# Linear attention into a gated Fourier filter: all inverse DFT tiles by one scheme, five output buffers and another order of work

## The chip, the cores and the metric

The kernel runs on one core of a Trainium2 chip. A core has a matrix engine (TensorE, PE in the profile; its weight loads are PEld), a vector engine (VectorE, DVE), a scalar engine (ScalarE, ACT), a general engine (GpSimd, POOL) and a queue engine (SyncE, SP) that here only issues DMAs. Each engine runs its instructions in the order in which it got them; between engines, semaphores hold an instruction back until its data is there or its buffer is free. PE writes into PSUM, eight banks of 128 x 512 fp32; DVE and ACT read it, POOL does not. The metric is the time of one execution in device microseconds: less is better.

## The reference

Eight batches with eight heads of 576 positions. The attention is linear: a feature map of exponentials, a sum over the keys, a quotient. Its output goes through three projections, one of which is convolved with a filter along the 576 positions (a product in the Fourier domain), and the gated product through a last projection.

```python
def phi(x):
    proj = np.einsum('bhsd,df->bhsf', x, w_phi)
    proj = proj - np.max(np.abs(proj), axis=-1, keepdims=True)
    return np.concatenate([np.exp(proj), np.exp(-proj)], axis=-1)
q_p, k_p = (phi(q), phi(k))
kv = np.einsum('bhsf,bhsd->bhfd', k_p, v)
z = np.sum(k_p, axis=2)
num = np.einsum('bhsf,bhfd->bhsd', q_p, kv)
den = np.einsum('bhsf,bhf->bhs', q_p, z)[..., None] + 1e-06
x = num / den                                   # -> [8, 576, 512]
...
proj = x @ w_proj                               # -> x1, x2, x3, 512 columns each
X2 = np.fft.rfft(x2, n=S, axis=1)
H = np.fft.rfft(filter_fft, n=S, axis=0)[None, :, :]
x2_conv = np.fft.irfft(X2 * H, n=S, axis=1)
y = x1 * x2_conv * x3
return (y @ w_out).astype(np.float32)
```

## The kernel before, in words

The whole order of work is written out by hand, as a text of some 1,480 words (`PLAN`, line 31). `run` (L1061) walks through it: each word names a method, its arguments (batch, tile, sometimes the engine) and, behind `@`, the first PSUM bank that it uses. No planner stands between: the words of one engine, in their order, are that engine's queue. A DMA stands in the queue of the engine that issues it: transposes (`trh`, `trx`, `trxt`) and nearly all stores (`st`) on SP, the loads of q, k, v and the weights (`load`, `loadh`, `w_load`) on POOL, between its arithmetic.

The batches run as a pipeline, several of them under way at a time. For one batch b:

- `load` brings q, k, v; `trh` transposes q and k by DMA. `Pk`, `Qn` (PE, L626, L633) project to the feature space, `maxk`, `maxq` (DVE, L707) take the largest absolute value, `ex` (ACT, L693) the two exponentials, `em` and `vs` (ACT L743; POOL or DVE L749) scale v. `Pq` projects q the other way round, `KV` (L753) sums over the keys, `NE` (L771) makes numerator and denominator, `rc` and `xn` (DVE, L792, L797) the quotient.
- `trx` transposes xn by DMA into xT for the projections. `f1` and `f2` (L844, L850) add and subtract its parts and `F` (L855) is the forward DFT into XF, copied out by `Fe`.
- `X2` (L892) projects in the Fourier domain, `Y1` (L899) multiplies by the filter into the tiles T0 to T4, `m3` (L909) adds two pairs of these.
- `X1`, `X3` (L940, L952) project in the position domain, `X1e` copies x1 out, `tm` (L958) multiplies by x3; the product stays in x1s.
- The inverse DFT goes by four tiles of 128 columns per batch, in one of two forms. `I` (L966) makes even and odd frequencies apart, three matmuls of 288 columns each, into two PSUM banks that stand side by side; `Ie` (ACT, L990) copies the first bank to SBUF (es), `Ip` and `Im` (DVE, L993) write the sum and the difference of es and the second bank to cv, and `ym` (L1038, POOL or DVE) multiplies cv by x1s into yT. `J` (L1021) makes the two halves of the result directly, five matmuls each, ten in all, for which it needs four further tables (`gen_neg`, `gen_ends`); `yj` (DVE, L1032) then multiplies both banks by x1s into yT in one instruction. 21 tiles go by I, 11 by J.
- `O` (L1046) is the last projection, by tiles c of a batch (c = 4 joins two batches), `Oe` copies it to an output buffer (o), and two `st` store that buffer's halves. `yt` (L1043) copies a remainder between two batches.

Buffers come in rings (`RING`, L25): a name with n buffers gives the n-th next writer the first buffer again, and it waits until its readers are done. `turn_of` (L228) hands out o, es and cv in the order in which the plan names their tiles: o has four buffers, es and cv two each. The words `wz` (L311) are matmuls on zeros, put where PE would otherwise stand still.

The end of the plan, with the last J, reads (L189 to L195):

```
X1e,ACT,7,1@5 Im,7,1@1 ym,POOL,7,0 J,7,2@6 tm,7,1@0 tm,7,2@4 ym,POOL,7,1 O,6,1@5 yj,7,2@6
Oe,ACT,6,1@5 O,7,2@6 yt,ACT,7 st,SP,6,1,1 O,7,1@7 Oe,ACT,7,2@6 st,SP,6,1,0 O,7,0@5 st,ACT,7,2,0
```

SP's queue around the second batch's transposes reads: `trh,q,4,1 st,0,0,0 trx,2,0 trx,2,1 trx,2,2 trx,2,3 trxt,2 st,0,3,0 st,0,3,1 st,0,0,1 trh,k,4,1 trh,q,4,0`. The output copies take their buffers in the order (0,3), (0,0), (0,1), (0,2), (1,0), (1,2), ...

Of the kernel before, what the change touches and what calls it, by code (L numbers as in the profile page):

```python
# [37 lines left out]
pt,k,0,0,1@3 sin,0 maxq,0,0@4 Pk,0,0@0 pte,ACT,k,0,0,1@3 pt,k,0,1,1@6 fa,POOL,1 pt,k,0,1,0@7
maxk,0,0@0 pte,ACT,k,0,1,1@6 Qn,0,2@4 pte,ACT,k,0,1,0@7 pte,DVE,q,0,1,1@2 maxq,0,2@4 Pk,0,1@6
Qn,0,3@2 ft,POOL fa,POOL,0 maxq,0,3@2 ex,k,m,0,0@0 wz,9@4 Qnt,0@4 ex,k,p,0,0@0 maxqt,0@4 Pk,0,2@2  # L40
maxk,0,2@2 ex,k,m,0,1@6 Pk,0,3@4 w_load,proj,1 rev@0 ex,k,p,0,1@6 maxk,0,3@4 mhi,0 ex,k,p,0,2@2
maxk,0,1@6 ex,k,m,0,2@2 one Pkt,0@6 mlo,DVE,0 ex,k,m,0,3@4 trm,0@2 wz,1@3 maxkt,0@6 trh,q,1,0
fb,0@0 trme,ACT,0@2 wz,12@3 em,m,0,0 ex,k,p,0,3@4 vs,POOL,m,0,0 Pq,0,1@2 trh,q,1,1 fb,1@0 em,p,0,0
exkt,m,0@6 Pq,0,2@4 exkt,p,0@6 ex,q,m,0,1@2 wz,25@0 trh,k,1,0 vs,POOL,p,0,0 ex,q,p,0,1@2 Qn,1,0@0
wz,14@6 trh,k,1,1 em,m,0,1 ex,q,p,0,2@4 maxq,1,0@0 Pq,0,3@2 w_load,proj,2 KV,0,0@6 ex,q,m,0,2@4
vs,DVE,m,0,1 em,p,0,1 ex,q,p,0,3@2 Ff,1@4 vs,POOL,p,0,1 KVe,DVE,0,0@6 Pk,1,1@0 ex,q,m,0,3@2
Ffe,DVE,1@4 Qn,1,3@6 ex,k,m,1,1@0 maxq,1,3@6 NE,0,1@4 Ff,0@2 w_load,proj,0 maxk,1,1@0 KV,0,1@6
Ffe,ACT,0@2 load,v,1 rc,0,1@4 ex,k,p,1,1@0 gen_ends,POOL Pq,0,0@2 xn,0,1@4 KVe,DVE,0,1@6 Qnt,1@4
trx,0,1 ex,q,m,0,0@2 Pk,1,0@0 maxqt,1@4 Ff,2@6 load,k,2 ex,q,p,0,0@2 maxk,1,0@0 NE,0,3@4 load,q,2
Ffe,ACT,2@6 NE,0,0@2 rc,0,3@4 ex,k,p,1,0@0 xn,0,3@4 NE,0,2@6 rc,0,0@2 Pqt,0@4 xn,0,0@2 ex,k,m,1,0@0  # L50
rc,0,2@6 ptx,0,3@2 f1,POOL,0,0,0 xn,0,2@6 exqt,p,0@4 ptx,0,0@3 Ff,3@0 exqt,m,0@4 ptxe,DVE,0,3@2
ptx,0,2@6 ptxe,DVE,0,0@3 f1,POOL,0,0,1 Ffe,ACT,3@0 Qn,1,2@4 ptxe,DVE,0,2@6 Pk,1,3@2 maxq,1,2@4
NEt,0@0 ex,k,m,1,3@2 f1,POOL,0,1,0 Pkt,1@6 exkt,m,1@6 rct,0@0 wz,27@4 maxk,1,3@2 f2,POOL,0,0,0
exkt,p,1@6 X1,0,0@5 Hl,ACT maxkt,1@6 H,0@4 f2,POOL,0,0,1 ex,k,p,1,3@2 xnt,0,0@0 H,2@6 xnt,0,1@0
He,DVE,0,0@4 f1,POOL,0,1,1 Qn,1,1@0 em,m,1,0 He,ACT,2,0@6 Pk,1,2@2 maxq,1,1@0 H,1@7 X1e,ACT,0,0@5
X1,0,3@6 ex,k,m,1,2@2 trh,k,2,0 He,DVE,0,1@4 X3,0,0@5 em,p,1,0 He,ACT,1,0@7 f2,DVE,0,1,1
vs,POOL,p,1,0 maxk,1,2@2 F,0,1@0 trh,k,2,1 X1e,ACT,0,3@6 X1,0,2@4 Fe,ACT,0,1@0 tm,0,0@5 H,4@6
em,m,1,1 f2,DVE,0,1,0 ex,k,p,1,2@2 X3,0,3@5 vs,POOL,m,1,0 X1e,DVE,0,2@4 trh,q,2,0 He,ACT,4,0@6
F,0,0@2 He,DVE,1,1@7 F,0,2@0 tm,0,3@5 Fe,ACT,0,0@2 H,3@4 trh,q,2,1 Fe,ACT,0,2@0 F,0,3@2
vs,POOL,m,1,1 He,ACT,3,1@4 Pk,2,0@0 KV,1,0@6 Fe,ACT,0,3@2 maxk,2,0@0 trxt,0 mhi,1 em,p,1,1  # L60
He,ACT,3,0@4 Pk,2,1@2 Xl,DVE,0 load,v,2 X2,0,2@5 ex,k,p,2,0@0 maxk,2,1@2 mlo,POOL,1 X2,0,1@4
KVe,ACT,1,0@6 load,q,3 late Y1,0,2@5 ex,k,p,2,1@2 trm,1@6 vs,POOL,p,1,1 X2,0,0@7 ex,k,m,2,0@0
trme,DVE,1@6 Y1,0,1@4 X2,0,4@5 ex,k,m,2,1@2 Pq,1,1@0 Y1,0,4@5 load,v,3 X2,0,3@4 ex,q,m,1,1@0
Y1,0,0@7 w_load,out Pkt,2@2 ex,q,p,1,1@0 X1,0,1@5 maxkt,2@2 load,k,3 Y1,0,3@4 X3,0,2@7 exkt,m,2@2
m3,POOL,0,0 exkt,p,2@2 Qn,2,1@0 X1e,ACT,0,1@5 tm,0,2@7 Pq,1,0@2 Pq,1,2@4 maxq,2,1@0 ex,q,m,1,0@2
X1t,0@7 X3t,0@6 ex,q,p,1,0@2 m3,DVE,0,1 X3,0,1@0 X1te,DVE,0@7 em,m,2,0 ex,q,p,1,2@4 tmt,0@6
NE,1,0@2 vs,POOL,m,2,0 tm,0,1@0 J,0,0@6 ex,q,m,1,2@4 rc,1,0@2 xn,1,0@2 NE,1,1@0 trx,1,0 yj,0,0@6
I,0,2@2 rc,1,1@0 Ie,0,2@2 I,0,1@6 xn,1,1@0 em,p,2,0 vs,POOL,p,2,0 Ie,0,1@6 Ip,0,2@2 trx,1,1
Pq,1,3@0 Im,0,1@6 KV,1,1@4 Im,0,2@2 ex,q,m,1,3@0 Ip,0,1@6 f1,DVE,1,0,1 Pk,2,2@6 ex,q,p,1,3@0
ym,POOL,0,1 J,0,3@2 maxk,2,2@6 KVe,ACT,1,1@4 NE,1,3@4 ym,POOL,0,2 ex,k,m,2,2@6 yj,0,3@2 NE,1,2@0  # L70
rc,1,3@4 KV,2,0@2 ex,k,p,2,2@6 rc,1,2@0 xn,1,3@4 f1,POOL,1,0,0 xn,1,2@0 trx,1,3 Pqt,1@6 Qn,2,0@4
exqt,m,1@6 f1,POOL,1,1,0 O,0,3@0 maxq,2,0@4 exqt,p,1@6 trx,1,2 O,0,0@1 KVe,ACT,2,0@2 f2,DVE,1,0,1
Oe,ACT,0,3@0 f1,DVE,1,1,1 Qn,2,3@2 trh,q,3,1 Oe,ACT,0,0@1 Qnt,2@4 f2,DVE,1,1,0 f2,POOL,1,1,1
NEt,1@6 maxq,2,3@2 O,0,1@1 trh,k,3,0 f2,POOL,1,0,0 rct,1@6 O,0,2@0 xnt,1,0@6 Oe,ACT,0,1@1 xnt,1,1@6
maxqt,2@4 Pk,2,3@2 trh,k,3,1 Oe,ACT,0,2@0 F,1,2@6 maxk,2,3@2 F,1,3@4 Fe,ACT,1,2@6 F,1,0@0 trh,q,3,0
Fe,ACT,1,3@4 X1,1,3@6 Fe,DVE,1,0@0 ex,k,m,2,3@2 Qn,2,2@4 st,SP,0,1,0 X1e,DVE,1,3@6 em,m,2,1 F,1,1@0
vs,POOL,m,2,1 trxt,1 maxq,2,2@4 X1,1,2@7 Fe,ACT,1,1@0 Qn,3,2@0 st,SP,0,1,1 mhi,2 X2,1,2@4
X1e,ACT,1,2@7 maxq,3,2@0 ex,k,p,2,3@2 load,q,4 X3,1,2@5 Y1,1,2@4 mlo,POOL,2 load,q,5 trm,2@2
X2,1,1@3 trme,ACT,2@2 em,p,2,1 tm,1,2@5 vs,POOL,p,2,1 Pq,2,0@1 Y1,1,1@3 Qn,3,0@4 Pq,2,1@6
ex,q,m,2,0@1 X3,1,3@0 maxq,3,0@4 ex,q,p,2,0@1 load,k,4 X1,1,0@3 ex,q,p,2,1@6 tm,1,3@0 Pq,2,2@4  # L80
ex,q,m,2,1@6 Pkt,3@0 X2,1,3@2 maxkt,3@0 X2,1,0@6 exkt,m,3@0 Y1,1,3@2 exkt,p,3@0 X1,1,1@7
ex,q,m,2,2@4 Y1,1,0@6 NE,2,1@0 X1e,ACT,1,1@7 X3,1,0@2 X1e,ACT,1,0@3 rc,2,1@0 m3,POOL,1,0 xn,2,1@0
ex,q,p,2,2@4 NE,2,0@6 tm,1,0@2 X1t,1@3 rc,2,0@6 Pqt,2@4 xn,2,0@6 X1te,ACT,1@3 Pq,2,3@0 exqt,p,2@4
Xl,DVE,1 Pk,3,1@2 f1,POOL,2,0,1 KV,2,1@6 trh,q,4,1 exqt,m,2@4 maxk,3,1@2 ex,q,p,2,3@0 f1,POOL,2,0,0
X2,1,4@4 st,SP,0,0,0 KVe,ACT,2,1@6 ex,q,m,2,3@0 trx,2,0 NE,2,2@6 m3,POOL,1,1 Y1,1,4@4 X3t,1@5
# [110 lines left out]
class Kernel:  # L196
# [807 lines left out]

    def gen_neg(self, eng):
        inv = self.at("inv")
        if eng == "ACT":
            self.nc.scalar.mul(inv[:, 6:8, :], inv[:, 2:4, :], -1.0)  # L1010
# [104 lines left out]
```

## Time and profile before

| | |
|---|---|
| median of 3 runs | 309.1 us (308.93 to 318.01) |
| span of the profiled execution | 311.6 us; no other time is given for this execution |
| busy in it: PE, DVE, ACT, POOL | 281.0, 268.6, 216.3, 203.8 us |
| mean granted clock of PE | 0.974 |
| moved by DMA | 40.2 MB |

The span runs from the first to the last instruction of one execution under the profiler. A row of a group names line, engine, operation, output and input tiles with their shapes and the count; behind the bar stand busy time and the mean of one in ns, and behind the second bar the idle time just before them and what ended it. A row of the timeline begins with start and length. A row of the chain of work has start, length and what it was. A row of the busy times by stage begins with its limits in us from the start. A matmul's length in a row is longer than what it takes of PE's time, since matmuls overlap in the array.

### The profile page before, as it was taken

The page shows a single profiled execution, that of the slowest core. Times are in us where ns is not written, and L with a number is a line of the kernel's source. Part 1 is how long each engine was busy: PE and PEld are TensorE (multiplying, and loading weights), DVE is VectorE, ACT ScalarE, POOL GpSimd, SP SyncE. Part 2 cuts the span into 40 slices and gives each one's busy share as a digit, 9 for nine tenths or more (in the row PEclk, how much of TensorE's full clock was granted, in tenths as well). Part 3 has the DMA queues.
Part 4 walks back from the last instruction along what each step waited for, and adds up shares of the span by engine and source line. Part 5 has one row for each costly group of instructions (what it writes and reads, how often), then busy time and mean ns, then how long its engine had stood idle before and what let it go on. Part 6 is the DMA issues. An engine that isn't in the chain of part 4 may idle for free.

```text
span 311.6 us, 10240 instructions
## 1 busy us (share of the span) xinstructions
PE 281.0 (90%) x4331; PEld 205.3 (66%) x4360; DVE 268.6 (86%) x447; ACT 216.3 (69%) x345; POOL 203.8 (65%) x163
## 2 busy tenths in 40 slices
...
GB/s 162 235 203 159 136 202 193 105 190 133 91 164 204 94 110 170 116 160 107 114 198 82 131 160 153 172 175 160 84 117 4 56 93 69 19 110 21 1 115 192
DMA packets 72735, 40.20 MB, mean 129 GB/s; under 512 B 53040, under 2 KB 67504, under 8 KB 72688
## 3 DMA queue, kind: packets, MB, share of 16 engines
q1 hardware_dynamic: 57472, 22.62, 40.2%
...
q14 instruction: 13, 0.11, 0.1%
...
## 4 chain that ended last, share of the span: by engine, by line
PE 70%; DVE 12%; DMA 7%; ACT 5%; issue 3%; SPq 1%; POOL 0%; DVEq 0%; POOLq 0%
PE ps L919 16%; PE ps L897 10%; PE ps L1049 8%; PE ps L764 5%; PE ps L972 4%; PE ps L778 4%; DMA xT<-xn 4%; DMA out_dram<-o 3%; PE ps L1028 3%; PE ps L858 3%; PE ps L862 3%; PE ps L928 2%; DVE mq L707 2%; PE ps L665 2%; PE ps L638 2%
## 5 line engine op out<-in xcount | busy, mean ns | idle before, releaser
L919 PE MATMUL ps<-xT,wproj 128*128 128x256 bf16 x512 | 65.8, 275 | 4.3 <-DVE x1s L960 2.3
L919 PEld LDWEIGHTS <-wproj 128*128 128x128 bf16 x512 | 48.6, 98 | 14.5 <-issue 5.1
L707 DVE TENSOR_REDUCE mk<-ps 128x8 f32<-128x1024 f32 (+1 forms) x40 | 44.0, 1110 | 5.9 <-ACT HTo L295 2.2
L707 DVE TENSOR_REDUCE mq<-ps 128x8 f32<-128x1024 f32 (+1 forms) x40 | 44.0, 1110 | 5.5 <-PE ps L638 4.5
L749 POOL TENSOR_TENSOR vm<-vn,vm 128x1152 bf16<-128x1152 bf16 x14 | 30.4, 2178 | 18.2 <-ACT vm L743 18.2
L749 POOL TENSOR_TENSOR vp<-vn,vp 128x1152 bf16<-128x1152 bf16 x16 | 34.8, 2180 | 10.5 <-ACT vp L743 10.3
L911 POOL TENSOR_TENSOR T<-T,T 128x1024 bf16<-128x1024 bf16 x12 | 25.5, 2124 | 21.9 <-DVE T L907 21.8
L693 ACT ACTIVATE Ekp<-ps 128x1024 bf16<-128x1024 f32 x32 | 32.8, 1030 | 6.6 <-DVE mk L707 3.3
L1038 POOL TENSOR_TENSOR yT<-cv,x1s 128x576 bf16<-128x576 f32 x19 | 24.3, 1289 | 18.3 <-DVE x1s L964 12.8
L852 POOL TENSOR_TENSOR xf<-SD 128x512 bf16<-128x512 bf16 x27 | 31.2, 1170 | 6.7 <-DVE SD L846 5.3
L693 ACT ACTIVATE Ekm<-ps 128x1024 bf16<-128x1024 f32 x32 | 32.8, 1033 | 3.6 <-DVE mk L707 2.7
L693 ACT ACTIVATE Eqm<-ps 128x1024 bf16<-128x1024 f32 x32 | 32.9, 1034 | 3.1 <-PE ps L671 2.9
L1049 PE MATMUL ps<-wout,yT 128*128 128x512 bf16 x133 | 34.3, 385 | 0.7 <-issue 0.2
L693 ACT ACTIVATE Eqp<-ps 128x1024 bf16<-128x1024 f32 x32 | 32.5, 1031 | 3.4 <-PE ps L671 3.3
L846 POOL TENSOR_TENSOR SD<-xn 128x512 bf16<-128x512 bf16 x23 | 26.5, 1160 | 12.6 <-DVE xn L797 12.6
L897 PE MATMUL ps<-wproj,XF 128*128 128x512 bf16 x117 | 30.3, 380 | 0.7 <-issue 0.2
L295 ACT CAST x1s<-ps 128x512 bf16<-128x512 f32 (+1 forms) x30 | 16.0, 548 | 13.1 <-PE ps L928 8.4
L797 DVE TENSOR_TENSOR xn<-ps,r 128x512 bf16<-128x512 f32 x32 | 22.0, 689 | 1.1
L1049 PEld LDWEIGHTS <-yT 128*128 128x128 bf16 x144 | 13.4, 99 | 14.1 <-issue 0.6
L990 ACT COPY es<-ps 128x288 f32<-128x288 f32 x21 | 8.5, 404 | 20.3 <-PE ps L972 19.8
L960 DVE TENSOR_TENSOR x1s<-ps,x1s 128x512 bf16<-128x512 f32 x32 | 21.7, 683 | 0.6 <-ACT x1s L295 0.4
L778 PE MATMUL ps<-KVs,Eqp 128*128 128x65 bf16 x256 | 19.6, 192 | 2.2 <-DVE mq L707 0.6
(174 smaller groups left out, 692.3 us busy)
## 6 DMA issues: line engine op xcount, KB each, us to landing
...
```

What stands on the lines that cost most here:

```text
L693: self.nc.scalar.activation(e, p, AF.Exp, bias=0.0, scale=1.0 if g == "p" else -1.0)
L707: self.nc.vector.tensor_reduce(out=out, in_=src, axis=AX.X, op=ALU.max, apply_absolute_value=True)
L749: self.eng(eng).tensor_tensor(out=t[:, :, :, 0:64], in0=self.at("vn", b)[:, 2 * X:2 * X + 2], in1=t[:, :, :, 64:65].to_broadcast([128, 2, ...
L778: self.mm(self.pb(u, 65 * a, 65 * a + 65), E, KVs[:, u, v, s, :], start=(s == 0), stop=(s == 1))
L797: self.nc.vector.tensor_tensor(out=o, in0=n[:, :, :, 0:64], in1=self.at("r", 4 * b + v).to_broadcast([128, 2, 4, 64]), op=ALU.mult)
L846: self.eng(eng).tensor_tensor(out=o[:, :, 2 * i:2 * i + 2, :], in0=x[:, :, 0:2, :], in1=x[:, :, 2:4, :], op=ALU.subtract if i else ALU.add)
L852: self.eng(eng).tensor_tensor(out=o[:, :, 2 * i:2 * i + 2, :], in0=x[:, :, 0:4:2, :], in1=x[:, :, 1:4:2, :], op=ALU.subtract if i else ALU ...
L897: self.mm(self.pb(0), l, w[:, kt, 512:1024], start=(kt == 0), stop=(kt == 3))
L911: self.eng(eng).tensor_tensor(out=Y, in0=Y, in1=self.at(f"T{2 * e + 1}", b), op=ALU.add)
L919: self.mm(o[:, d], w[:, kt, f0 + 128 * m:f0 + 128 * m + 128], y[:, 1, ::-1, ::-1] if d else y[:, 0], start=(kt == 0), stop=(kt == 3))
L1038: self.eng(eng).tensor_tensor(out=self.at("yT", b)[:, m, 0:SEQ], in0=self.turn_of("cv", (b, m)).rearrange("p x h t -> p (x h t)"), in1=sel ...
L1049: self.mm(self.pb(0), y[:, kt, 128 * c:128 * c + 128], w[:, kt, :], start=(kt == 0), stop=(kt == 3))
```

## The change

All 32 inverse tiles go by I: J, yj and the two methods that make its tables go, `inv` shrinks from ten tables to six, and o gets a fifth buffer (four tables are 2,304 bytes of a partition, one such buffer 2,048). The plan is written anew: many words stand elsewhere, have other PSUM banks or another engine. The counts of words that change: I, Ie, Ip, Im 21 to 32; J, yj 11 to 0; gen_neg, gen_ends 1 to 0; ym on POOL 19 to 25, on DVE 2 to 7; Fe on ACT 26 to 20, on DVE 6 to 12; Oe on ACT 19 to 28, on DVE 17 to 8; X1e on ACT 24 to 26, on DVE 8 to 6; X1te on ACT 6 to 7; Xl on DVE 3 to 4; f1 on POOL 23 to 25, on DVE 9 to 7; f2 on POOL 27 to 26, on DVE 5 to 6; vs on POOL 30 to 31, on DVE 2 to 1; mlo on POOL 5 to 6; Ffe on DVE 1 to 2.

```diff
-RING = {..., 'r': 4, 'o': 4, 'kn': 2, ...}
+RING = {..., 'r': 4, 'o': 5, 'kn': 2, ...}
...
-X1e,ACT,7,1@5 Im,7,1@1 ym,POOL,7,0 J,7,2@6 tm,7,1@0 tm,7,2@4 ym,POOL,7,1 O,6,1@5 yj,7,2@6
-Oe,ACT,6,1@5 O,7,2@6 yt,ACT,7 st,SP,6,1,1 O,7,1@7 Oe,ACT,7,2@6 st,SP,6,1,0 O,7,0@5 st,ACT,7,2,0
...
+trh,k,4,0 st,SP,0,2,1 st,SP,0,3,0 st,SP,0,1,0 trx,2,1 trx,2,0 trh,q,4,1 trh,k,4,1 trx,2,2 trx,2,3
+trxt,2 st,SP,0,0,0 trh,q,4,0 st,SP,0,1,1 I,1,3@2 Pk,3,2@4 Pk,3,0@0 Ie,1,3@2 ex,k,m,3,2@4
...
+maxk,3,2@4 X1,2,1@3 O,1,0@2 Qn,3,3@6 F,2,0@0 O,1,2@4 yt,ACT,1 Oe,ACT,1,0@2 Fe,ACT,2,0@0 Oe,ACT,1,2@4
+X1e,DVE,2,1@3 maxq,3,3@6 Pk,3,3@0 X1,2,2@5 F,2,3@6 maxk,3,3@0 Fe,DVE,2,3@6 F,2,2@2 Fe,DVE,2,2@2
+O,1,3@4 F,2,1@6 Fe,DVE,2,1@6 em,m,3,0 em,p,3,0 X1e,ACT,2,2@5 ex,k,m,3,3@0 em,m,3,1 ex,k,p,3,3@0
...
+Y1,7,4@0 X2,7,3@1 Y1,7,3@1 O,6,2@3 X3,7,3@2 Oe,ACT,6,2@3 O,6,3@1 m3,DVE,7,1 tm,7,3@2 I,7,3@5
+Ie,7,3@5 Ip,7,3@5 Im,7,3@5 ym,POOL,7,3 I,7,1@3 Ie,7,1@3 Oe,ACT,6,3@1 Ip,7,1@3 Im,7,1@3 ym,DVE,7,1
+X1,7,2@2 I,7,0@0 Ie,7,0@0 I,7,2@5 Ie,7,2@5 X1e,ACT,7,2@2 X3,7,2@3 O,6,0@4 Oe,ACT,6,0@4 st,SP,5,0,0
+st,SP,5,1,1 st,SP,6,3,1 st,SP,6,3,0 st,SP,6,2,0 st,SP,6,2,1 st,SP,6,0,0 O,6,1@7 Oe,ACT,6,1@7
+st,SP,6,0,1 st,SP,6,1,1 st,SP,6,1,0 Ip,7,0@0 Im,7,0@0 ym,POOL,7,0 Ip,7,2@5 tm,7,2@3 Im,7,2@5
+ym,DVE,7,2 O,7,1@0 Oe,DVE,7,1@0 yt,DVE,7 O,7,2@3 Oe,ACT,7,2@3 st,ACT,7,1,0 st,ACT,7,2,0 O,7,3@1
+Oe,DVE,7,3@1 st,ACT,7,3,1 st,SP,7,1,1 st,SP,7,2,1 st,SP,7,3,0 O,7,0@7 Oe,ACT,7,0@7 st,ACT,7,0,1
+st,SP,7,0,0 O,7,4@2 Oe,DVE,7,4@2 st,ACT,7,4,0 st,SP,7,4,1
...
-        R("inv", [128, 10, 288], BF16)
+        R("inv", [128, 6, 288], BF16)
...
-    def gen_neg(self, eng):
...
-    def gen_ends(self, eng):
...
-    def J(self, b, m):
...
-    def yj(self, b, m):
```

The new plan's output copies take their buffers in the order (0,3), (0,0), (0,2), (0,1), (1,0), (1,2), (1,3), ... SP's stores of (0,3) stand ahead of `trx,2,1`, the first store of (0,0) right behind `trxt,2`.

333 lines of the change are left out of this document (151 added, 182 removed).

## The prediction

> **What bounds the kernel now.** I read the page first, then the busy time by stages (cut where the work changes character), then the chain of work and the timeline around the longest stops.
>
> ```profile
> span 311.6 us, 10240 instructions
> PE 281.0 (90%) x4331; PEld 205.3 (66%) x4360; DVE 268.6 (86%) x447; ACT 216.3 (69%) x345; POOL 203.8 (65%) x163
> PE 70%; DVE 12%; DMA 7%; ACT 5%; issue 3%; SPq 1%; POOL 0%; DVEq 0%; POOLq 0%
> ...
> 60.00:203.00 143.00, 135.82 (x2107) 99.38 (x2123) 122.83 (x181) 108.37 (x171) 102.17 (x76) 0.99 0.91 142
> 203.00:220.00 17.00, 15.97 (x359) 13.51 (x354) 15.38 (x28) 10.38 (x17) 12.30 (x9) 1.00 0.94 152
> 220.00:291.00 71.00, 70.00 (x1093) 51.73 (x1095) 67.19 (x105) 47.56 (x78) 45.79 (x31) 1.00 0.31 61
> 291.00:311.60 20.60, 15.05 (x116) 10.55 (x112) 11.21 (x21) 3.65 (x8) 3.80 (x3) 0.94 0.45 117
> 0.00:60.00 60.00, 44.13 (x682) 30.13 (x687) 51.97 (x116) 46.29 (x76) 39.71 (x45) 0.91 1.02 176
> ```
>
> The stage rows give, in order, length, then busy time of PE, PEld, DVE, ACT and POOL, the granted clock, the DMA share and GB/s. PE carries 70% of the chain that ends last. From 60 to 291 us it is busy 221.8 of 231, so a matmul that goes there is time that goes, unless another engine is as full. One is, late: from 220 to 291 DVE is busy 67.2 of 71, against 122.8 of 143 before. ACT and POOL have a third free. The first 60 us are bound by loads and DVE's tables, the last 20 by the output's own latency.
>
> **The change, part by part.**
>
> *Six matmuls for ten.* The diff turns 11 J into I; both stand in the chain of work, with what each takes of PE's time (start, length):
>
> ```profile
> 180.04 1.23 PE ps L1028 x10
> 181.27 0.73 PE ps L972 x6
> ```
>
> 1.23 - 0.73 = 0.50 us per tile, 11 tiles: -5.5 us of PE. Of the 11, three lie after 203 us in stages that DVE shares, one of them in the tail. For the rest PE was the limit.
>
> *What that puts on the other engines.* Rows of the groups (busy, mean ns of one); I divide busy by count, as neighbours overlap a little.
>
> ```profile
> L993 DVE TENSOR_TENSOR cv<-es,ps 128x288 f32<-128x288 f32 x42 | 17.3, 446 | 4.2 <-ACT es L990 3.8
> L1032 DVE TENSOR_TENSOR yT<-ps,x1s 128x576 bf16<-128x576 f32 x11 | 8.3, 753 | 0.7 <-PE ps L1028 0.2
> L1038 DVE TENSOR_TENSOR yT<-cv,x1s 128x576 bf16<-128x576 f32 x2 | 1.5, 753 | 0.0
> L297 DVE CAST XF<-ps 128x576 bf16<-128x576 f32 x6 | 4.5, 752 | 0.9 <-PE ps L862 0.9
> L297 DVE COPY o<-ps 128x512 f32<-128x512 f32 x17 | 11.4, 684 | 5.9 <-DMA out_dram<-o 3.4 <-PE ps L1049 2.4
> L297 DVE CAST x1s<-ps 128x512 bf16<-128x512 f32 x8 | 5.5, 682 | 0.1
> L846 DVE TENSOR_TENSOR SD<-xn 128x512 bf16<-128x512 bf16 x9 | 6.2, 695 | 0.2
> L749 DVE TENSOR_TENSOR vm<-vn,vm 128x1152 bf16<-128x1152 bf16 x2 | 2.8, 1411 | 0.0
> L990 ACT COPY es<-ps 128x288 f32<-128x288 f32 x21 | 8.5, 404 | 20.3 <-PE ps L972 19.8 <-DVE xn L797 0.3
> L295 ACT COPY o<-ps 128x512 f32<-128x512 f32 x19 | 11.3, 594 | 11.3 <-PE ps L1049 9.8 <-issue 1.3
> L295 ACT CAST XF<-ps 128x576 bf16<-128x576 f32 x26 | 16.1, 642 | 7.4 <-PE ps L862 7.3
> L1038 POOL TENSOR_TENSOR yT<-cv,x1s 128x576 bf16<-128x576 f32 x19 | 24.3, 1289 | 18.3 <-DVE x1s L964 12.8 <-DVE cv L993 5.4
> ```
>
> Counting the plan's words on each side, DVE gets 22 more half sums (22 x 0.41 = +9.1) and 5 more ym (5 x 0.75 = +3.8) for 11 yj less (-8.3), 6 more Fe (+4.5), 9 Oe less (9 x 0.67 = -6.0), and 2 X1e, 2 f1 and 1 vs less (2 x 0.68 + 2 x 0.69 + 1.41 = -4.1). That is -1.0; the single instructions moved besides come to under 1 either way. So DVE stays at some 268 us. ACT gets 11 es and 9 Oe and loses 6 Fe: 4.4 + 5.3 - 3.7 = +6.0; POOL gets 6 ym, 6 x 1.28 = +7.7, and one vs more. Both hide in idle time (ACT 95, POOL 108 us in the span) as long as the work arrives in time; if that cover went, the whole 6 or 8 us would be late. DVE has no such cover after 203: three J lie there, and I count 1.0 us of their 1.5 as not gained. The dropped tables' one ACT and two POOL instructions lie in the first 60 us, where neither is the limit: nothing.
>
> *A fifth output buffer.* The longest stop of the steady part is at 118 us. Timeline and stages of 2 us:
>
> ```profile
> 113.32 7.04 DMA out_dram<-o
> ...
> 120.46 0.69 DVE L297 COPY o<-ps 128x512 f32<-128x512 f32 x1 [2.99 <-DMA out_dram<-o]
> 121.20 0.28 PE L858 MATMUL ps<-Dt,xnt 128*128 128x288 bf16 x1 [2.38 <-DVE o L297]
> ...
> 118.00:120.00 2.00, 0.81 (x9) 0.57 (x8) 0.00 (x0) 1.02 (x2) 2.00 (x2) 1.00 1.17 200
> 120.00:122.00 2.00, 0.58 (x6) 0.50 (x7) 1.54 (x2) 0.00 (x0) 1.28 (x1) 0.89 1.27 257
> 122.00:124.00 2.00, 2.00 (x8) 1.00 (x8) 1.54 (x3) 1.32 (x2) 0.00 (x0) 0.50 0.45 109
> 124.00:126.00 2.00, 2.00 (x25) 1.52 (x24) 0.92 (x1) 1.31 (x3) 0.15 (x1) 0.75 0.02 3
> ```
>
> Oe of tile (1,2) is the sixth to take an output buffer; with four it needs the store of (0,0), which SP issues third behind trxt,2 and which takes 7.04 us to land. DVE stands 2.99 us, behind it maxk and Fe, and PE, which needs their banks, misses 2.6 of the 4 us from 118. Then the clock is down: (1 - 0.50) x 2 + (1 - 0.75) x 2 + 0.1 = 1.6 us. Together 4.2. With five, (1,0) takes the new buffer and (1,2) that of (0,3), whose stores stand before trx,2,1; the store of (0,0) is awaited only by (1,3), one Pk, one X1 and two F later, on ACT. The gain lies between 0 (the same stop one tile later) and 4.2; I take 4.2, as its first store after trxt,2 is now the one needed and some 2 us of work lie between.
>
> The Trainium skill ("TensorE: Matmul & The Clock Gate", section "What's actually happening") says that the clock halves after an idle window of about 3.4 us. By that rule a stop of 2.6 would not have lowered it, and this part would be worth 2.6, the sum 1.6 more; the rows above show 0.50 right behind the stop, and I go by them.
>
> *The tail.*
>
> ```profile
> 296.79 0.40 ACT L990 COPY es<-ps 128x288 f32<-128x288 f32 x1 [3.87 <-PE ps L972]
> ...
> 191.58 0.87 PE ps L919 x8
> 130.14 0.86 PE ps L1049 x4
> L960 DVE TENSOR_TENSOR x1s<-ps,x1s 128x512 bf16<-128x512 f32 x32 | 21.7, 683 | 0.6 <-ACT x1s L295 0.4 <-PE ps L919 0.2
> 300.62 5.49 PE L1049 MATMUL ps<-wout,yT 128*128 128x512 bf16 x23
> 306.50 0.69 DVE L297 COPY o<-ps 128x512 f32<-128x512 f32 x1 [0.41 <-DMA out_dram<-o]
> ```
>
> The last output tiles need the whole last yT. After the change, from the start of I,7,3, PE has four I, two projections and O,6,0 and O,6,1: 4 x 0.73 + 2 x 0.87 + 2 x 0.86 = 6.4 us. DVE's chain to the last ym is I and es (0.73 + 0.40), eight half sums (3.3), two ym (1.5) and one tm (0.68): 6.6. So PE waits 0.2, and with hand-overs 0.6, where it now waits 0.3 (5.49 for six tiles of 0.86): +0.3. The last copy's wait for a buffer goes: -0.4.
>
> *The new order.* SP's and POOL's queues are reshuffled (trh,q,4,1 now stands between trx,2,0 and trx,2,2; loads of q come later on POOL; ym,0,3 stands ahead of f1,1,1,0). The trace cannot price this. Bounds: outside the stop above PE idles 7.2 - 2.6 + 1.0 + 1.0 = 6.6 us from 60 to 291; all of it could go, or as much be added. I take 0, the middle, since the same instructions in the same stages fill the same queues; the start (16 us of PE idle, same work) I leave alone too.
>
> Sum: -5.5 + 1.0 - 4.2 + 0.3 - 0.4 = -8.8; 311.6 - 8.8 = 302.8. The profiled span is 2.5 us above the median of 309.1 of the plain runs, which holds for both kernels: **300.3 us**.
>
> **Rivals.**
> - *DVE keeps the time.* If DVE's 268 us set the pace everywhere, PE's 5.5 us turn into waits. Against it: PE idles only 7.2 of 143 us before 203, DVE 20. For it: DVE at 95% after 220. Only the ring and the tail are left: 311.6 - 4.2 - 0.4 + 0.3 - 2.5 = 304.8.
> - *The clock loss belongs to something else* (the skill's rule above): 300.3 + 1.6 = 301.9.
> - *Slower: the bank pairs wait in DVE's queue.* A J pair is free after one yj; an I pair only after es on ACT and two half sums in DVE's order, and the next matmuls into it wait.
>
> ```profile
> DVE cv L993 <- ACT es L990: 3.8, 5, 1.3
> ```
>
> The five waits of DVE for es come to 3.8 us, the longest 1.3. If each of the 11 new tiles stops DVE for 1.3 and PE with it, that is 14.3, and with the clock lost as at 118 (1.6 for 2.6) 23.1: 300.3 + 23.1 = 323.4. It decides from 8.8 us, 0.50 per new tile. Against it: 16 of 21 such tiles cost nothing.
> - *All stops go.* The new order clears the other 6.6 us of PE idle: 293.7.
>
> That the change doesn't do what it says is not open: J's code is gone and the plan has 32 I.
>
> **How the numbers follow.** Forecast 0.52 (own range 297 to 305), DVE 0.18, clock 0.04, slower 0.14, all stops gone 0.12. About 2% is what a measurement of this kernel can tell from no change: 302.9 and 315.3. Faster: three quarters of the forecast, 0.12 and half of the clock's case, 0.53. Slower: the part of that rival above 315.3 (over 0.84 us per tile), 0.11. Same: 0.36. The range from 293 to 315 leaves out half of the best case and that upper part, 0.17.
>
> **What would show it.** Right: 192 inverse matmuls at L972 and none of J, PE's busy time near 275; no DVE copy of o waiting for a store at 118 and no 0.50 clock behind it; DVE's busy time within 2 of 268.6; PE's idle time from 60 to 291 below 8. Wrong: waits of PE on DVE's half sums, DVE above 97% from 220, or PE stops over 2.6 us elsewhere, above all on xT behind a late load in SP's queue.

## The result, and the profile after

The kernel after takes 333.0 us (median of four runs, 332.24 to 334.47); the kernel before, beside it on the same chip, 310.1. The ratio is **1.0746, 95% interval 1.0702 to 1.0791**: 7.5% slower, where the prediction said 300.3 us and 293 to 315. Ratios leave disturbed executions out and medians do not, so the two can differ by a per cent; here both say the same.

The page of the kernel after (span; busy time of the engines; the chain that ended last), and its busy time by the stages of the prediction (limits, then PE, PEld, DVE, ACT, POOL, granted clock, DMA share, GB/s):

```profile
span 330.3 us, 10236 instructions
PE 286.9 (87%) x4316; PEld 203.6 (62%) x4316; DVE 280.6 (85%) x456; ACT 220.6 (67%) x359; POOL 214.5 (65%) x170
q8 instruction: 33, 0.54, 0.7%
PE 51%; DMA 17%; DVE 16%; issue 6%; ACT 4%; SPq 3%; POOL 2%; DVEq 0%; ACTq 0%; POOLq 0%
```

```profile
0.00:60.00 60.00, 39.61 (x536) 25.05 (x537) 44.94 (x106) 37.97 (x58) 35.26 (x41) 0.77 1.12 179
60.00:203.00 143.00, 135.44 (x2164) 99.01 (x2164) 129.89 (x194) 108.82 (x181) 107.58 (x81) 0.99 0.79 129
203.00:220.00 17.00, 12.06 (x219) 7.32 (x213) 14.88 (x12) 8.89 (x13) 12.04 (x7) 0.90 1.08 182
220.00:291.00 71.00, 66.59 (x1096) 48.91 (x1097) 63.73 (x97) 52.75 (x86) 46.56 (x32) 1.00 0.29 53
```

PE's part of the chain fell from 70% to 51%, DMA's rose from 7% to 17%. Two stages stand out: the first 60 us (PE busy 39.6 where it was 44.1, clock 0.77 where it was 0.91) and 203 to 220 (12.1 where it was 16.0). To place the loss, here is when `xn` of some tiles starts (us, from the traces), with four of the runs told below:

| | xn,1,0 | xn,3,0 | xn,4,2 | xn,5,0 | xn,7,0 | span |
|---|---|---|---|---|---|---|
| before | 70.8 | 138.2 | 176.9 | 206.6 | 269.6 | 311.6 |
| after | 82.8 | 147.8 | 184.6 | 222.5 | 287.5 | 330.3 |
| loads | 73.4 | 138.7 | 176.9 | 214.9 | 279.9 | 323.0 |
| loads_xl4_v7 | 73.7 | 138.7 | 174.8 | 209.2 | 273.6 | 316.8 |
| six_early | 68.6 | 137.9 | 176.4 | 213.5 | 276.4 | 318.1 |
| before_o5 | 71.5 | 134.5 | 172.9 | 201.8 | 265.0 | 306.9 |

After loses 12 us by batch 1, wins 4 back by batch 4, loses 8 in front of batch 5, and 3 more by the end.

*The start.* The chain of work of the kernel after, in order of time (start, length, what):

```profile
7.27 6.80 DMA fl<-in_moe_filter_fft_dram
14.48 2.34 POOL turn L490
16.82 0.73 POOL vn L592
17.55 10.26 DMA kn<-in_k_dram
27.82 10.24 DMA kT<-kn
38.10 0.63 PE ps L633 x8
...
40.71 14.09 DMA xT<-xn
54.84 1.65 PE ps L921 x7
```

On POOL the new plan has `fa,POOL,0 load,v,0 load,k,1`. `fa` waits for the filter's DMA; so k of batch 1 is issued at 17.55 and its transpose lands at 38.06. `Pk,1,1` (L633) stands in PE's queue and holds everything behind it. So the transpose of xn is issued at 40.71, where the kernel before has it at 36.70, and it takes 14.09 us, not 8.74. One matmul of the first X1 runs ahead of that (50.39; before, 44.41); the seven that wait for this transpose start at 54.84, not at 45.47 as before.

*Batch 5.* Timeline of DVE, POOL and PE of the kernel after (start, length; in brackets the idle time before and what ended it):

```profile
204.30 5.89 DVE L299 COPY XL<-XF 128x512 bf16<-128x512 bf16 x1
...
201.57 4.26 POOL L751 TENSOR_TENSOR vp<-vn,vp 128x1152 bf16<-128x1152 bf16 x2
205.78 4.25 POOL L751 TENSOR_TENSOR vm<-vn,vm 128x1152 bf16<-128x1152 bf16 x2
...
212.50 0.30 PE L667 MATMUL ps<-qT,wphi 64*128 64x256 bf16 x2 [4.34 <-DVE T L909]
220.86 0.20 PE L766 MATMUL ps<-vm,Ekm 64*128 64x65 bf16 x1 [1.46 <-issue]
```

A DVE copy from SBUF to SBUF, 0.28 us where the kernel before has a copy of this shape on DVE (that of batch 4 was on ACT), lasts 5.89, until POOL's run of four products has ended at 210.0; PE stops 4.34 us behind it, and 1.46 more for nothing that the profile names. That such records account for DVE's surplus is seen in the groups (busy, mean ns), of after and of before:

```profile
L299 DVE COPY XL<-XF 128x512 bf16<-128x512 bf16 x4 | 8.4, 2110 | 0.0
L913 DVE TENSOR_TENSOR T<-T,T 128x1024 bf16<-128x1024 bf16 x4 | 7.6, 1906 | 0.0
```

```profile
L297 DVE COPY XL<-XF 128x512 bf16<-128x512 bf16 x3 | 0.8, 282 | 0.0
L911 DVE TENSOR_TENSOR T<-T,T 128x1024 bf16<-128x1024 bf16 x4 | 3.3, 835 | 0.1
```

(8.4 - 0.8) + (7.6 - 3.3) = 11.9 us, and DVE's busy time is 280.6 - 268.6 = 12.0 above that of the kernel before, at which the forecast had left it.

### The profile page after: what moved, and what is told of

Read it like the earlier page. It is cut to its first block, busy times and chain, and to the rows that moved or that the text cites. A ratio compares the mean times of both kernels' runs of the same rounds, so it can differ in the third digit from the quotient of the medians.

```text
span 330.3 us, 10236 instructions
## 1 busy us (share of the span) xinstructions
PE 286.9 (87%) x4316; PEld 203.6 (62%) x4316; DVE 280.6 (85%) x456; ACT 220.6 (67%) x359; POOL 214.5 (65%) x170
## 4 chain that ended last, share of the span: by engine, by line
PE 51%; DMA 17%; DVE 16%; issue 6%; ACT 4%; SPq 3%; POOL 2%; DVEq 0%; ACTq 0%; POOLq 0%
PE ps L921 12%; PE ps L899 7%; PE ps L1021 7%; DMA xT<-xn 5%; PE ps L766 4%; PE ps L974 4%; DMA out_dram<-o 4%; DVE mq L709 3%; DMA kn<-in_k_dram 3%; DMA kT<-kn 3%; PE ps L780 3%; DVE T L909 2%; PE ps L667 2%; DMA fl<-in_moe_filter_fft_dram 2%; DVE mk L709 2%
## 5 line engine op out<-in xcount | busy, mean ns | idle before, releaser
L921 PE MATMUL ps<-xT,wproj 128*128 128x256 bf16 x512 | 67.0, 277 | 7.0 <-DMA xT<-xn 5.5
L1010 POOL TENSOR_TENSOR yT<-cv,x1s 128x576 bf16<-128x576 f32 x25 | 33.0, 1331 | 23.0 <-DVE cv L995 22.6
L848 POOL TENSOR_TENSOR SD<-xn 128x512 bf16<-128x512 bf16 x25 | 29.0, 1172 | 17.3 <-DVE xn L799 17.3
L695 ACT ACTIVATE Eqm<-ps 128x1024 bf16<-128x1024 f32 x32 | 32.7, 1033 | 10.2 <-PE ps L673 8.8
L751 POOL TENSOR_TENSOR vm<-vn,vm 128x1152 bf16<-128x1152 bf16 x15 | 33.3, 2227 | 9.1 <-ACT vm L745 5.7
L1021 PE MATMUL ps<-wout,yT 128*128 128x512 bf16 x144 | 35.6, 386 | 1.6 <-ACT o L297 0.8
L899 PE MATMUL ps<-wproj,XF 128*128 128x512 bf16 x128 | 32.1, 380 | 0.0
L297 ACT CAST x1s<-ps 128x512 bf16<-128x512 f32 (+1 forms) x33 | 17.8, 551 | 21.0 <-PE ps L921 18.1
L974 PE MATMUL ps<-inv,T 128*128 128x288 bf16 x192 | 29.3, 294 | 1.3 <-DVE x1s L962 0.8
L995 DVE TENSOR_TENSOR cv<-es,ps 128x288 f32<-128x288 f32 x64 | 25.8, 445 | 3.0 <-ACT es L992 1.7
L992 ACT COPY es<-ps 128x288 f32<-128x288 f32 x32 | 12.7, 403 | 19.6 <-PE ps L974 15.2
```

The lines of the kernel that those rows point to most:

```text
L695: self.nc.scalar.activation(e, p, AF.Exp, bias=0.0, scale=1.0 if g == "p" else -1.0)
L751: self.eng(eng).tensor_tensor(out=t[:, :, :, 0:64], in0=self.at("vn", b)[:, 2 * X:2 * X + 2], in1=t[:, :, :, 64:65].to_broadcast([128, 2, ...
L848: self.eng(eng).tensor_tensor(out=o[:, :, 2 * i:2 * i + 2, :], in0=x[:, :, 0:2, :], in1=x[:, :, 2:4, :], op=ALU.subtract if i else ALU.add)
L899: self.mm(self.pb(0), l, w[:, kt, 512:1024], start=(kt == 0), stop=(kt == 3))
L921: self.mm(o[:, d], w[:, kt, f0 + 128 * m:f0 + 128 * m + 128], y[:, 1, ::-1, ::-1] if d else y[:, 0], start=(kt == 0), stop=(kt == 3))
L974: self.mm(self.pb(e, 0, 288), l, inv[:, 2 * e + i if i < 2 else 4 + e, :], start=(i == 0), stop=(i == 2))
```

## The experiments

Line numbers in the variants are shifted by a few. Ratios are to the kernel before, run beside each on the same chip. The runs were made on several chips: the kernel before has a median of 313.4 us beside loads_xl4, loads_xl4_k7, j_back_o5 and six_dve, and of 310.1 to 311.8 beside the others. A few us between runs of different groups can come from there.

### The start: loads

```diff
-maxq,0,1@2 fa,POOL,0 load,v,0 load,k,1 fa,POOL,1 ...
+maxq,0,1@2 load,v,0 load,k,1 fa,POOL,0 fa,POOL,1 ...
```

> The kernel after, with two words moved: on GpSimd the loads of k,1 and v,0 are issued ahead of fa,0, which waits for the filter's DMA, and not behind it. Theory S (the lost time begins in the start: k,1 is issued 10 us late, kT of it lands at 38.06, the first X1 starts at 54.84 where before it started at 45.47): kn is issued by 8 us, the first X1 starts at 45 to 48, and of the 9.4 us of lag some 9 are gone from the end, 322 to 326 us. Rival W (the stretches behind are bound by VectorE or by the added half sums, the late start is absorbed in them): the first X1 is early and the time stays at 331 to 334.

Measured: 324.8 us, ratio 1.0531 (1.0431 to 1.0631). Timeline of POOL, and of PE at the first X1:

```profile
7.05 0.76 POOL L596 DMA_DIRECT2D vn<-in_v_dram  x1
7.80 0.75 POOL L596 DMA_DIRECT2D kn<-in_k_dram  x1
14.21 4.66 POOL L494 TENSOR_TENSOR turn<-fl 128x1024 f32<-128x1024 f32 x2 [5.65 <-DVE mq L713]
...
46.25 0.92 PE L925 MATMUL ps<-xT,wproj 128*128 128x256 bf16 x7 [1.15 <-DMA xT<-xn]
```

The seven matmuls of the first X1 start at 46.25, and at the end 8.2 us are gone by the medians, 7.3 by the profiled spans (330.3 to 323.0): theory S, in its range. Two words in POOL's queue are the largest single cause that was found.

### VectorE beside GpSimd: port, xl_before, loads_xl4

```diff
port (on after):
-Xl,DVE,0 ... Xl,DVE,1 ... Xl,DVE,4 ... m3,DVE,0,1 ... m3,POOL,0,0
+Xl,ACT,0 ... Xl,ACT,1 ... Xl,ACT,4 ... m3,POOL,0,0 m3,POOL,0,1
xl_before (on before):
-Xl,ACT,4
+Xl,DVE,4
loads_xl4 (on loads):
-Xl,DVE,4
+Xl,ACT,4
```

> The kernel after, with Xl of batches 0, 1 and 4 on ScalarE where VectorE had them, and m3,0,1 on GpSimd behind m3,0,0. Theory P (these VectorE instructions, which read and write SBUF alone, last until GpSimd's run of instructions beside them ends: 5.89 us for a copy that takes 0.28, 3.91 for an m3 that takes 0.7, 1.77 for another copy; TensorE stops behind them): XL's copy at about 204 us takes 0.6 us on ScalarE, the VectorE stops at 73 to 81 and 204 to 210 are gone, 326 to 330 us. Rival Q (the records only look long because the instruction waits for its input in the engine, or the time comes back in the stretch behind): 332 to 334. Theory S takes no side.

> The kernel before, with one word changed: the copy Xl of batch 4 goes from ScalarE (0.61 us, at 197.5 us) to VectorE, where it falls beside GpSimd's two vm products of 196.95 to 201.2. Theory P: VectorE's copy, 0.28 us with GpSimd idle, lasts until GpSimd's run ends, 2 to 4.5 us, and the time grows by 1 to 4 us. Rival Q: the copy takes 0.3 to 0.6 us beside GpSimd as well, and the time stays within 1 us of 310.

port: 333.4 us, 1.0705 (1.0558 to 1.0853), nothing won. xl_before: 311.1, 1.0003 (0.9943 to 1.0062). Both miss what theory P expected; the times are those of rival Q. Timeline of port, and then of xl_before:

```profile
81.11 3.35 DVE L1014 TENSOR_TENSOR yT<-cv,x1s 128x576 bf16<-128x576 f32 x1
...
219.55 0.20 PE L770 MATMUL ps<-vm,Ekm 64*128 64x65 bf16 x1 [4.71 <-issue]
```

```profile
196.00 0.80 DVE L299 COPY XL<-XF 128x512 bf16<-128x512 bf16 x1
...
194.51 4.31 POOL L751 TENSOR_TENSOR vm<-vn,vm 128x1152 bf16<-128x1152 bf16 x2
```

In port the long copies are gone, but other stops stand in their place: at 81 a DVE product of two SBUF tiles (0.75 us in the kernel before) lasts 3.35 beside POOL's products, and in batch 5 PE stops 4.71 us with no named wait. In xl_before the copy lasts 0.80, not 2 to 4.5: it ended at the seam between POOL's two products (196.66), not at the run's end. So the block is real, but its length is between the rest of one product and that of a whole run. The Trainium skill ("GPSIMD Engine Reference", section "Specifications") says that GpSimd and VectorE share their SBUF interfaces, with contention for DVE instructions in a 2-port mode or with two SBUF inputs; the rows agree, and 0.28 against 5.89 us is its size here.

> The run loads (k,1 and v,0 issued ahead of fa,0) with the copy Xl of batch 4 on ScalarE. In loads that copy lay on VectorE from 196.72 for 5.88 us beside four GpSimd products, and TensorE stopped 4.3 us behind it and 1.5 us for no wait that the profile names. Theory P (the copy alone makes the stop): the stops go, 318 to 321 us. Theory F (TensorE's next 16 KB of code is late as well: the instruction queue's packet came at 210.94 in loads, 19 us after the one before, between the loads v,6, k,7, v,7, the transposes and the stores): a stop without a named wait, 3 to 5 us, takes the copy's place, 323 to 326 us.

loads_xl4: 321.6 us, 1.0242 (1.015 to 1.0335), the copy 0.6 us on ACT, and

```profile
211.23 0.20 PE L770 MATMUL ps<-vm,Ekm 64*128 64x65 bf16 x1 [3.49 <-issue]
```

a 3.49 us stop in the copy's place, as theory F said. The time does not decide: it lies between the two ranges, and the medians of loads and loads_xl4 differ by 3.3 us, the ratios by 2.9%, on two chips and with a per cent of interval each.

### The stop without a name: loads_xl4_k7, loads_xl4_v7, six_dve_v7, before_v7

```diff
loads_xl4_k7 (on loads_xl4): load,k,7 from behind load,v,6 to behind load,q,7
loads_xl4_v7 (on loads_xl4), six_dve_v7 (on six_dve, below), before_v7 (on before):
-... vs,POOL,m,5,1 load,v,7 m3,POOL,4,1 ... f2,POOL,5,1,1 ...
+... vs,POOL,m,5,1 m3,POOL,4,1 ... f2,POOL,5,1,1 load,v,7 ...
```

> The run loads_xl4 with load k,7 moved ahead on GpSimd, from behind load v,6 to behind load q,7 (some 10 us earlier). Theory F: with the two loads apart TensorE's code comes in time, the stop without a named wait at about 210 is under 1.5 us, 317 to 321 us. Rival: the stop stays at 3 us or more, 323 to 326 us; then the loads are not what the code waits for.

322.3 us, 1.0284 (1.019 to 1.0378): a miss, the stop was 4.76 us. The DMA view of this run for 207.5 to 208.5 us (queue, kind: packets, MB, share of 16 engines) has

```profile
q8 instruction: 1, 0.02, 5.9%
```

and that for 191.5 to 207.5 has no packet of q8 at all. By its count q8 is TensorE's code: 33 packets of 16 KB in the page above for 4,316 matmuls and as many weight loads, 262 instructions a packet. Between the packet at 190.7 and the stop PE issued 259 matmuls and 258 weight loads, two blocks. The next packet came 17 us behind the last, when the load v,7, issued at 202.00, had run out.

> The run loads_xl4 with the load v,7 issued later on GpSimd, behind f2,5,1,1 (some 20 us) and not behind the four products of v,5. In loads_xl4_k7 TensorE's code packet came at 207.96, in the same 2 us in which the packets of that load (issued at 202.00) ended, and TensorE stood 4.8 us until then. Theory F2 (the code waits behind this load of 576 KB): the packet comes by 204, the stop without a named wait is under 1 us, 4 us less than loads_xl4, 315 to 318 us. Rival (the stop has another cause, or the time comes back): stop of 3 us or more, or 320 to 323 us.

> The run six_dve (order of before, 11 tiles as six matmuls, the added products on VectorE) with load v,7 issued some 20 us later. There TensorE stood 3.2 us at 204 to 207 and its code came at 207.39. Theory F2: that stop goes and the time falls by 3 to 5 us; up to 177 us this kernel ran 1 to 2 us ahead of the one before, so some 314 to 318 are left for VectorE's added 9 us. Rival: 319 us or more.

> The kernel before with load v,7 issued some 20 us later. Its code packets came at 200.67, 208.97 and 212.86 and TensorE never ran out there (stops without a named wait: 0.4 us at 200 to 235). Theory F2: nothing to win, within 1.5 us of the kernel before. Rival (the load slows the transposes and stores beside it as well): 2 to 4 us faster than the kernel before.

loads_xl4_v7: **317.9 us, 1.0196** (1.0097 to 1.0295), the stop 1.0 us. six_dve_v7: 321.7, 1.0329 (1.0237 to 1.0421), its stop 0.5 us where it was 3.2. before_v7: 312.5 against 311.8, 1.0124 (1.0053 to 1.0194): nothing won, if anything lost. The stops do what theory F2 says. The times show it less well: loads_xl4_v7 is in F2's range, but its ratio's interval overlaps that of loads_xl4, and six_dve_v7 is in the rival's range. Its ratio is that of six_dve (1.0316), and its profiled span is no shorter (320.0 against 319.0); a wait of PE for half sums at the forward DFT behind the stop has grown from 1.4 to 2.2 us. So that the late code stops PE is shown, and that the whole stop is won when it goes is not.

Counted in the traces, this stop stands before the 2,912th weight load, whichever order the kernel follows (us):

| | 2,784th weight load | code packet | 2,912th weight load | v,7 issued |
|---|---|---|---|---|
| loads_xl4_k7 | 203.2 | 208.0 | 210.2 | 202.0 |
| loads_xl4 | 205.5 | 208.9 | 211.2 | 204.2 |
| six_early | 206.4 | 209.0 | 211.4 | 204.9 |
| loads_xl4_v7 | 204.3 | 205.1 | 207.6 | 218.2 |
| six_dve_v7 | 206.8 | 207.2 | 209.6 | 220.6 |

128 matmuls (256 instructions) lie between the two loads and take 2 us in KV. PE goes on 2.2 to 2.5 us after the packet, whenever it comes; the packet comes 0.4 to 0.8 us after the first of them without the load v,7 and 2.6 to 4.8 us with it. That it is asked for there is inferred from these numbers. The kernel before has the same delay without the stop: the packet behind its own 2,912th weight load (204.6) came at 209.0 with v,7 in flight (201.50 to 208.9), and in before_v7 0.8 us behind that load (204.7 and 205.5). Its PE stood 0.4 us at most there, so little was to be won. It does have a stop without a name, of 1.6 us at 178.4, before the 2,528th weight load: three times 128 ahead of the 2,912th.

### Where the blocks end: loads_xl4_pad, before_pad

```diff
+    def pad(self, n):
+        z = self.at("zz")
+        for _ in range(n):
+            self.mm(self.pb(0, 0, 16), z[:, 0:128], z[:, 0:16], True, True)
loads_xl4_pad (on loads_xl4): pad,28@4 behind wz,9@4
before_pad (on before): pad,100@1 behind wz,26@1
```

> The run loads_xl4 with 28 small matmuls on zeros (128 weights, 16 columns, their result unused) more on TensorE in the start, and nothing else. In the five kernels with a stop without a named wait inside KV,5 it stood before the same weight load, the 2912th, in either order: a block of code ends there, and the next block is asked for 128 matmuls ahead, 2 us in this stretch. 28 matmuls are what seven six-matmul tiles took away ahead of that place, so the blocks end where they ended in the kernel before. Theory F3 (where the blocks end decides): the stop of 3.5 us at KV,5 is under 1.5 us and the time falls to 317 to 319 us. Rival (the stop belongs to the load v,7 or to KV's work, wherever the blocks end): the stop stays at 3 us, 321 to 323 us.

> The kernel before with 100 such matmuls more in the start (28 and 100 are 128: one block of code), so that its blocks end where those of the kernels with six-matmul tiles end. Theory F3: TensorE now stops 2 to 4 us for no named wait inside KV,5 at about 205 us, where the kernel before has 0.4 us in that stretch, and the time grows by 3 to 6 us, beside 0 to 3 us that the added matmuls may take in the start. Rival: no such stop, and no more than the start's 0 to 3 us.

loads_xl4_pad: 321.0 us, 1.0286 (1.0191 to 1.0381), no faster than loads_xl4 by the ratio. before_pad: 316.5, 1.0284 (1.021 to 1.0358). The waits of PE from 195 to 225 us (waiter, releaser: us, times, longest) in loads_xl4_pad and in before_pad:

```profile
PE ps L983 <- issue: 2.1, 1, 2.1
```

```profile
PE ps L771 <- issue: 1.5, 1, 1.5
```

The count does set the place: the stop left KV,5 in loads_xl4_pad and came into it in before_pad (0.4 us there in the kernel before), in both before the 3,040th weight load, 128 behind the other. But it did not go: it is 2.1 us in the inverse DFT (L983), and one of 2.1 us is new at 85.5 us, before the 1,120th weight load (14 times 128 ahead of the 2,912th). In this execution `xn,4,2` to `xn,5,0` takes 31.5 us, against 35.6 in loads_xl4; the ratios show no gain from it. And before_pad's price was mis-sized: `xn,4,2` (178.6) to `xn,5,0` (210.5) takes 31.9 us where before took 29.7. Of its other loss 5.5 us are there at `xn,1,0` (76.3). Part of that can be the added matmuls, and part has a reason that nobody had put in: in this execution the copy XL of batch 0 met a product of POOL. DVE's timeline in before_pad, and in before_o5 for comparison:

```profile
61.03 2.70 DVE L299 COPY XL<-XF 128x512 bf16<-128x512 bf16 x1
```

```profile
60.07 0.28 DVE L299 COPY XL<-XF 128x512 bf16<-128x512 bf16 x1
```

The old order has this trap too: 2.70 us in before_pad, before_v7, six_o4 and six_early_o5, 0.28 in the kernel before, xl_before, before_o5, six_dve, six_dve_v7 and six_early. `xn,1,0` starts at 73.4 to 76.3 in the first four and at 68.6 to 71.5 in the others. It is a matter of which comes first at 59 us, so a comparison of two profiles of this order can be off by some us on its account; how often the plain runs fall in it was not measured.

### The stop at 63 to 72 us: fixes

```diff
-Xl,DVE,0 ... m3,DVE,0,1 ... m3,POOL,0,0 ... ym,DVE,0,0
+Xl,ACT,0 ... m3,POOL,0,0 m3,POOL,0,1 ... ym,POOL,0,0
```

> The run loads_xl4_v7 with Xl of batch 0 on ScalarE, m3,0,1 and ym,0,0 on GpSimd, so that no VectorE instruction that reads and writes SBUF alone lies beside GpSimd's products at 62 to 72 us (1.77 and 3.91 us there in loads, with a TensorE stop of 2.5 behind them). Theory P: that stop goes, 2 to 3 us less than loads_xl4_v7. Rival R (what an engine gains there is given back in front of xT's transposes, as in port, which won nothing): within 1.5 us of loads_xl4_v7.

On loads_xl4_v7: 318.5 us, 1.024 (1.0156 to 1.0323). `xn,1,0` starts 4.1 us earlier (69.6), `xn,3,0` at 138.5 as in loads_xl4_v7. Rival R: what is won ahead of batch 2 is lost before batch 3.

### The tiles alone: six_o4, six_dve, six_early, j_back_o5, late_j

```diff
six_o4 (on before), for each of the 11 J tiles; gen_neg, gen_ends and their tables go:
-J,b,m@k ... yj,b,m@k
+I,b,m@k Ie,b,m@k ... Ip,b,m@k Im,b,m@k ym,POOL,b,m
six_dve: ym,DVE for ym,POOL in these tiles
six_early: as six_dve, but 4,0 4,3 5,0 and 7,2 stay J
j_back_o5 (on after): the reverse for the 11 tiles
late_j (on loads_xl4_v7): the reverse for 4,0 4,3 5,0 and 7,2
```

> The kernel before in its own order, banks and engines, with its 11 ten-matmul tiles turned into six matmuls, ScalarE's copy, two half sums and a product (on GpSimd, for batch 7 on VectorE), no tables made, o still four buffers. Theory O (the arithmetic is worth what was forecast, 4.5 us, and the searched order is what costs): 303 to 308 us. Rival V (the added half sums and copies cost more than the matmuls save, pairs of PSUM banks wait for them in VectorE's queue): 314 to 324 us.

> The run six_o4 (330.9 us: the order of before, 11 tiles as six matmuls) with the 11 added products on VectorE, right behind their half sums, where six_o4 had ten of them on GpSimd. GpSimd's queue is then that of the kernel before without gen_ends. Theory G (six_o4 lost its time in GpSimd's queue: v's products, f1, f2 and yT late behind the added products): 308 to 316 us. Rival D (VectorE cannot take 9 us more in that order: its half sums and the product are on the path): 322 to 332 us. Had the forecast's sum held for the tile alone, 304 to 306.

> The run six_dve with the last four of the 11 tiles (4,0, 4,3, 5,0 and 7,2) as ten matmuls again, in the words of the kernel before; the seven tiles of batches 0 to 3 stay six matmuls. Theory L (six_dve's loss lies with the four late tiles, where VectorE is full: it is 1 us ahead at 176 and 8 behind at 282): 308 to 313 us, at or below the kernel before; the forecast's 0.5 us a tile would be 3.5. Rival E (each tile costs, wherever it lies): 316 to 320 us.

six_o4: 330.9 us, 1.0697 (1.0609 to 1.0785). six_dve: 326.0, 1.0316 (1.0197 to 1.0435). six_early: 321.9, 1.0437 (1.036 to 1.0515). In the old order the tile makes the kernel slower, on either engine, and seven tiles do so nearly as much as eleven: theories O, G and L fall. Of L one thing is seen: from `xn,5,0` to `xn,7,0` six_early takes 62.9 us, like the kernel before (63.0), where six_dve takes 65.9. Where the rest goes, the waits of PE from 45 to 190 us in six_early show in part:

```profile
PE ps L923 <- DVE x1s L964: 2.3, 1, 2.3
PE ps L923 <- DMA xT<-xn: 2.3, 3, 0.8
PE ps L635 <- DVE cv L997: 2.1, 2, 1.8
PE ps L1053 <- DVE yT L1042: 2.0, 1, 2.0
PE ps L669 <- DVE xn L801: 1.1, 1, 1.1
```

The waits on the half sums (cv) and on a product (yT), 4.1 us, are new; the kernel before has 2.4 us on its copy to o instead. By `xn,4,2` seven tiles have won 0.5 us (176.4 against 176.9) where the forecast had 3.5. Then six_early loses 7.4 us up to `xn,5,0`. The stretch in six_early, and in the kernel before:

```profile
176.40:213.50 37.10, 30.98 (x438) 21.55 (x437) 26.81 (x41) 24.28 (x40) 23.89 (x17) 0.88 0.95 149
```

```profile
176.90:206.60 29.70, 28.12 (x454) 20.65 (x457) 24.99 (x37) 22.91 (x37) 22.79 (x17) 1.00 0.99 159
```

PE idles 6.1 us there and not 1.6: 2.7 on the stop of TensorE's code, 2.3 on half sums (1.8 of them in the third row above), 0.8 on xT. And it is busy 2.9 us longer for no more matmuls, at a granted clock of 0.88 where it was 1.00.

> The kernel after with its order, banks, engines and five o buffers, but the same 11 tiles as in the kernel before as ten matmuls and one VectorE product, with the tables that they need. Theory O (the order costs, and the six-matmul tile is worth 4.5 us): 334 to 340 us. Rival V (the six-matmul tile costs: its half sums, copies and products fill the engines): 312 to 326 us.

> The run loads_xl4_v7 (the order after with its three stops mended, 317.9 us) with the tiles 4,0, 4,3, 5,0 and 7,2 as ten matmuls and one VectorE product (gen_neg and gen_ends put in behind batch 1). Theory L (six-matmul tiles cost where VectorE is full): 312 to 316 us. Rival O (what is left against the kernel before is the order's, not the tiles'): 317 to 321 us.

j_back_o5: 344.9 us, 1.0989 (1.0896 to 1.1082), even above theory O's range. It is no clean price: with the old tables made in the new start, `xn,1,0` is at 85.6, 2.8 us later than in after, and PE has another stop without a named wait, of 5.4 us, before the 3,040th weight load; the code packet came at 233.2, the load v,7 was in flight from 220.98 to 232.9. late_j: 320.3, 1.0388 (1.032 to 1.0456): rival O, the late tiles are not what keeps loads_xl4_v7 above the kernel before. So either half of the change alone, as run here, is slower than the kernel before, and the halves do not add up.

### The fifth buffer: before_o5, six_early_o5

```diff
-'o': 4
+'o': 5
```

> The kernel before with five o buffers and nothing else changed. The prediction's term: the TensorE stop of 2.4 us at 118 (behind VectorE's copy to o, which waits for a store) goes, with the clock's loss behind it 4.2 us, 306 to 308. Rival (the 4 us that batch 1 gains come back before batch 3, whose start other waits set): the stop goes and the time stays within 1.5 us of the kernel before.

> The run six_early with five o buffers. If the prediction's two terms hold, each in its place, 304 to 307 us, faster than both kernels. If the ring's gain comes back, as six_early.

before_o5: 309.0 us against 310.9, ratio **1.0010 (0.9955 to 1.0064)**. Its busy time by stages of 2 us, where the kernel before had PE at 0.81 and 0.58 and the clock at 0.50:

```profile
118.00:120.00 2.00, 1.95 (x20) 1.59 (x20) 2.00 (x3) 1.66 (x4) 2.00 (x2) 1.00 1.15 167
120.00:122.00 2.00, 2.00 (x27) 1.46 (x25) 1.47 (x3) 2.00 (x4) 1.99 (x1) 1.00 1.31 261
122.00:124.00 2.00, 2.00 (x12) 0.88 (x10) 2.00 (x4) 1.05 (x5) 1.61 (x1) 1.00 0.48 121
```

The stop and the lost clock are gone, and in this execution the 4.0 us hold from `xn,4,2` to the end. In the times they do not show: by the interval at most 0.45%, 1.4 us, is won. Why the timed runs do not keep what the profiled one keeps stays open. Two things bear on it. The profiled execution of the kernel before is a long one, 311.6 us by its span against a plain median of 309.1. And the clock does not fall behind every such stop: in before_v7 PE stops 2.1 us at the same copy, and the clock stays at 1.00:

```profile
122.00:124.00 2.00, 0.51 (x6) 0.44 (x6) 1.25 (x2) 0.00 (x0) 1.88 (x1) 1.00 1.27 257
124.00:126.00 2.00, 1.71 (x23) 1.12 (x20) 1.83 (x3) 1.40 (x3) 0.00 (x0) 1.00 0.60 134
```

In xl_before it is 0.54 and 0.61 in the two stages behind a stop of 2.3 us. six_early_o5: 325.5, 1.0492 (1.0389 to 1.0596), no gain; its copy XL of batch 0 is one of the 2.70 us ones, so it says little of the buffer. No version beat the kernel before.

## Why the prediction was wrong, point by point

1. **The new order, taken at 0: the step that failed.** "The trace cannot price this", with 6.6 us either way from PE's idle time of before. Idle time bounds what an order can win, not what it can lose. Three places in it were mended with four words: POOL's loads behind `fa`, the copy XL beside POOL's products, the load v,7 beside TensorE's code. They took the kernel from 333.0 to 317.9 us, the ratio from 1.0746 to 1.0531, 1.0242 and 1.0196. The first is some 7 to 8 us; the split of the other two is within the intervals, and in the profiles they are worth 3.6 us together in their place (`xn,4,2` to `xn,5,0` takes 38.0 in loads, 34.4 in loads_xl4_v7). That the start, "same work", was left alone was the worst line: the same words stood in another order in POOL's queue, and 7 to 8 us hung on two of them. Both that order and POOL's run `vs,p,5,0 vs,p,5,1 vs,m,5,0 vs,m,5,1` beside `Xl,DVE,4` could be read in the diff.
2. **Six matmuls for ten, -5.5 + 1.0.** The 192 matmuls at L974 are there and J is gone, but in the old order seven tiles won 0.5 us by batch 4, not 3.5: PE waited for the half sums and products. That is the rival "DVE keeps the time", at work before 203 us too, where I had DVE's free time as cover. The slower rival put a tile's price at 1.3 us of stop, with the clock's loss on top; in six_early seven cost 1.6 each by the medians (10.9 us), 1.9 by the ratio. That this is near is in part luck. Of the 7.4 us between `xn,4,2` and `xn,5,0` (37.1 against 29.7) PE's waits for half sums are 2.3, which is that rival's mechanism, and the lower clock is its second half; but 2.7 are TensorE's late code, which nobody had put in.
3. **DVE stays at 268.6.** 280.6. The count of instructions was right; 11.9 of the 12.0 too many are XL and m3, lengthened by POOL.
4. **The fifth buffer, -4.2.** Right in its place (the DVE copy waits for no store, the clock is 1.00 behind it, 4.0 us ahead in the profile), not confirmed in the time (1.4 us at most). Its 1.6 us of clock are no sure part of the stop: before_v7 has the stop without them.
5. **The clock.** The rule of the Trainium skill ("TensorE: Matmul & The Clock Gate", section "What's actually happening"), an idle window of about 3.4 us, was set against the row. The clock fell behind a stop of 2.4 us in the kernel before behind one of 2.3 us in xl_before and behind one of 2.0 us in six_early (0.53 from 116 to 118), and before_o5, without the stop, has 1.00. So the loss did belong to that stop, and an idle time below 3.4 us was enough. Behind 2.1 us in before_v7 it did not come: the length of a stop alone does not decide it here.
6. **The tail, -0.1.** `xn,7,0` to the end takes 42.8 us after and 42.0 before: the wrong sign, by less than a us.
7. **The signs named.** "PE stops over 2.6 us elsewhere, above all on xT behind a late load" was the right alarm (4.2 us on xT at 54.84); the load was late on POOL, not SP. Of the signs of being right, the 192 inverse matmuls came. PE's busy time is 286.9 us and not 275, at a mean clock of 0.946 where it was 0.974, and it idles 16.9 us from 60 to 291, not under 8.
8. **The step from span to median, -2.5.** It was to hold for both kernels. The profiled execution of the kernel after has a span of 330.3 us, 2.7 below its plain median. So 5.2 us of the 32.7 between 300.3 and 333.0 are this term, and not the change.

Open: the last 6 us between loads_xl4_v7 and the kernel before (2% by the ratio, 1.0 to 3.0). They build up from batch 5 on (174.8 against 176.9 at `xn,4,2`, 209.2 against 206.6 at `xn,5,0`, 273.6 against 269.6 at `xn,7,0`); late_j and fixes did not find them. The largest step, 4.7 us, is `xn,4,2` to `xn,5,0` (34.4 against 29.7): there PE waits 2.0 us on the transpose into xT in loads_xl4_v7 and not in the kernel before, and the clock is 0.95 and not 1.00. In loads_xl4_pad, without that wait and at 1.00, the stretch takes 31.5. What makes the wait was not tested.
